# A fused linear-attention and gated-MLP kernel: another hand-written order of its operations, other queues for the first loads, and the last output block in two halves

## The chip, the cores and the metric

The kernel runs on one core of one Trainium2 chip. The metric is the time of one execution on the device in microseconds (us). An engine's name is followed by the short form that the profile uses: TensorE (PE; its weight loads PEld), VectorE (DVE), ScalarE (ACT), GpSimd (POOL) and SyncE (SP), which only issues DMAs.

## The reference

Inputs are float32: q, k, v of 8 batches x 8 heads x 576 tokens x 64, a feature matrix w_phi (64 x 128), and the MLP's weights w_in (512 x 1024), w_spatial (576 x 576), b_spatial and w_out (512 x 512).

```python
def phi(x):
    proj = np.einsum('bhsd,df->bhsf', x, w_phi)
    proj = proj - np.max(np.abs(proj), axis=-1, keepdims=True)
    return np.concatenate([np.exp(proj), np.exp(-proj)], axis=-1)
kv = np.einsum('bhsf,bhsd->bhfd', phi(k), v)
z = np.sum(phi(k), axis=2)
x = np.einsum('bhsf,bhfd->bhsd', phi(q), kv) / (np.einsum('bhsf,bhf->bhs', phi(q), z)[..., None] + 1e-06)
# heads side by side: x is batch x 576 x 512
h = np.maximum(x @ w_in, 0.0)
u, v = h[..., :512], h[..., 512:]
v_n = (v - mean(v)) / np.sqrt(var(v) + 1e-06)
v_s = np.einsum('ts,bsd->btd', w_spatial, v_n) + b_spatial[None, :, None]
out = (u * v_s) @ w_out
```

## The kernel before

A batch's 576 tokens are cut into 512 (four rows per partition, one descriptor each) and a tail of 64; the tails of two batches share 128 partitions. Every step is a small function (marked `@op`) named by a few letters; `ORDER` (line 17) is a text of some 1400 words, and the program is written out in just that order. A word such as `tkc.0.1.1:1@A` names the function, its arguments (batch, half or quarter, part), the buffer or PSUM bank after the colon, and the engine after the @ (A is ACT, V is DVE, P is POOL, S is SP). So the text alone decides what each engine does, in which order, in which of the buffers of `BUFS` (line 147), and which engine makes a copy; the framework adds the semaphores. Engines run their own rows strictly in order.

A batch goes through these steps.

- Loads: `lk` and `lq` (L358, L362) fetch k and q on POOL's queue, with the cast to bfloat16 on the way; `lv` (L388) fetches v on SP's queue, `lkt`, `lqt`, `lvt` (L271) the tails. Batch 0's k comes as four quarters of two heads each, in float32 (`lkf`, L348), each cast by `ckf` (L257) on DVE or POOL; its q comes as two halves (`lq0`, L372).
- Turning: `tk`, `tq` (L488) transpose on TensorE through PSUM, and `tkc`, `tqc` (L257 on DVE and POOL, L255 on ACT) copy the result to the tile T. Later batches use transposing DMAs instead (`xk`, `xq`, L474).
- Maxima: `kp`, `qp` (L540) multiply by w_phi, tokens on partitions; `km`, `qm` (L545, DVE) take the largest absolute value of each row and head.
- Features: `ke` (L549, ACT) takes the exponential of the key's product with both signs, `kem` and `kee` (L554) the exponential of the maxima; `vs` (L605, mostly POOL) multiplies v by the latter, and `kv` (L640, L642) sums on TensorE. For q the maxima are split into two bfloat16 (`qs`, L657, POOL), turned (`qt`, L662), copied (`qc`), and subtracted on TensorE while the product is made again (`qf`, L666, L670); `qe` (L675, ACT) takes the exponentials, `qn` (L724) multiplies by the sums and `qr`, `qx` (L730, L737, DVE) divide.
- MLP: x is turned (`tx`, L807, or `xx`, L800), `vm` and `um` (L839, L937) are the products with w_in, `vr`, `ur` their relu on ACT or DVE (L261, L263), `vb`, `va`, `vw`, `vn` the normalization, `sm` (L952, L954) the product along the tokens, `sg` (L961, DVE) the gate, `om` (L966) the product with w_out, `oc` (L255 or L257) the copy out of PSUM and `od` (L977) the store of one block of 128 tokens.
- `warm` (L334) issues matmuls whose result nobody reads; 35 of them stand in the first stages.

Batches overlap: products of the MLP of one batch stand between the attention of the next ones.

Of the kernel before, what the change touches and what calls it, by code (L numbers as in the profile page):

```python
# [53 lines left out]
kp.2.3:2,3 vnt.0.0:0@P kp.2.2:6,7 qp.3.0.1:0,1 vst.1.1.1:0@P qm.3.0.1:0 um.1.2:5 xk.3.0:5@S vm.1.3:4 ke.2.3.0:0
xk.3.1:3@S ke.2.2.0:3 km.2.3:3 km.2.2 vn.0.2@P xq.4.0:6@S ur.1.2:2@A vr.1.3:2@A ke.2.3.1 kee.2.0:2 vst.1.0.1@P tqt.1:0
vm.1.0:1 qt.2.1:4 qc.2.1:1@V vst.1.0.0@P tqtc.1:0@V spt.4:5 ke.2.2.1 vb.1.3:0 vr.1.0:1@A qp.3.1.0:2,3 vm.1.2:4
kee.2.1:3 qf.2.1.0:6,7 qf.2.1.1:0,1 vr.1.2:0@A qm.3.1.0:3 lk.4:0 vs.2.2.1:1@P spc.4@V qpt.1:2,3 qe.2.1.0.1:0
qe.2.1.0.0 sm.0.2:4 qmt.1:1 qe.2.1.1.1:4 qe.2.1.1.0 sm.0.3:5 vs.2.0.0:0@P sg.0.2 lout qp.3.0.0:2,3 qf.2.0.0:6,7
vsz.2.0@P vsz.2.2@P xq.4.1:1@S vbt.0.1:1 sm.0.1:4 qe.2.0.0.0:1 sg.0.3 qe.2.0.0.1 um.1.1:5 ur.1.1@A vb.1.0:3 qm.3.0.0
vb.1.2:2 qf.2.0.1:0,1 vsz.2.1:2@P vstz.1@P vs.2.2.0@P vs.2.3.1:3@P kp.3.0:2,3 qe.2.0.1.0:2 qp.3.1.1:6,7 sg.0.1  # L60
km.3.0:0 kv.2.2:5 kvc.2.2:2@V qe.2.0.1.1 vs.2.1.0@P qm.3.1.1 um.1.0:4 kp.3.1:0,1 km.3.1 um.1.3:5 ur.1.0@V ke.3.0.1:1
vat.0.1:2 qs.3.0:2@P vs.2.3.0@P sm.0.0:6 ke.3.0.0 vs.2.1.1@P vsz.2.3@P ur.1.3@A qt.3.0:7 qc.3.0:0@V kv.2.3:2 kv.2.1:3
ke.3.1.0:3 sg.0.0 ke.3.1.1 qp.4.0.0:4,5 vs.2.0.1@P vb.1.1:1 qs.3.1:0@P qst.1:2@P kp.3.2:6,7 kee.3.0:0 kvc.2.3@V
vsz.3.0:1@P kp.3.3:0,1 qm.4.0.0:2 smt.0.0:2 kvc.2.1@A vst.1.1.0@P lq.5:1 om.0.2:3 ke.3.2.0:0 sgt.0.0 ke.3.2.1 qt.3.1:2
qc.3.1:1@A qtt.1:4 kv.2.0:5 vs.3.0.0@P km.3.3:2 oc.0.2:0@A om.0.3:2 km.3.2 ke.3.3.0:2 qct.1:2@A kvc.2.0@V om.0.0:3
ke.3.3.1 oc.0.3:1@V qp.4.1.0:6,7 qf.3.0.0:4,5 lkt.2:1@S qn.2.0.0:0,1 oc.0.0:2@A qm.4.1.0:0 qr.2.0.0:1 va.1.2:3
xk.4.0:2@S qx.2.0.0:0 qn.2.1.0:2,3 vs.3.0.1@P qft.1:6,7 vs.3.1.0:3@P qn.2.0.1:0,1 vxt.0.1@V qr.2.1.0:2 vs.3.1.1@P
va.1.0 qe.3.0.0.0:3 qe.3.0.0.1 va.1.3 qx.2.1.0:1 va.1.1 ckt.2:0@P lk.5:2 qet.1.0:1 lv.4.0:1@S qet.1.1 qr.2.0.1:0
vx.1.2@V kee.3.1:3 qx.2.0.1 vsz.3.1@P qn.2.1.1:4,5 om.0.1:2 tx.2.1:3 qp.4.1.1:0,1 vy.1.2@V oc.0.1:3@A qr.2.1.1:1
txc.2.1:2@A xk.4.1:5@S qx.2.1.1 qm.4.1.1 vyt.0.1@V qf.3.0.1:6,7 qe.3.0.1.1:0 qp.4.0.1:4,5 qm.4.0.1 kv.3.0:2  # L70
vs.3.3.1:2@P vm.2.1:3 tx.2.2:0 tx.2.0:1 qe.3.0.1.0 kvc.3.0:0@V txc.2.2@A kp.4.0:4,5 ke.4.0.0:4 vw.1.2:2@P vn.1.2:2@P
vn.1.3@P vn.1.1@P qf.3.1.0:6,7 vr.2.1:0@V txc.2.0@V tkt.2:0 tx.2.3:2 txc.2.3@V vs.3.2.1:0@P qe.3.1.0.1:2 vm.2.2:1
qe.3.1.0.0 tktc.2:0@V vwt.0.1:3@P vsz.3.2@P vs.3.3.0@P km.4.0:1 vn.1.0@P vr.2.2:2@V vnt.0.1@P vm.2.0:2 vr.2.0:3@A
kv.3.1:0 ke.4.0.1 kp.4.2:6,7 kvc.3.1@A qf.3.1.1:2,3 vb.2.2:2 lv.4.1:3@S vb.2.0:3 vb.2.1:0 qs.4.1:0@P qe.3.1.1.1:4
lk.6:0 lvt.2:0@S vm.2.3:1 vs.3.2.0@P km.4.2:3 um.2.1:0 od.0.3@S vr.2.3:1@A qe.3.1.1.0 qs.4.0:2@P vsz.3.3@P smt.0.1:4
sgt.0.1 va.2.1:4 va.2.2 lv.5.1:0@S ur.2.1:0@V sm.1.2:1 kp.4.3:4,5 sg.1.2 kp.4.1:2,3 xq.5.1:3@S kv.3.2:0 km.4.3
# [75 lines left out]
def kernel(  # L152
# [16 lines left out]
    nc = tc.nc  # L169
# [5 lines left out]
    P = 128  # L175
# [886 lines left out]
```

## Time and profile before

| | us |
|---|---|
| median of 3 runs (lowest and highest) | 258.46 (257.28 to 258.59) |
| profiled execution | 259.11 |
| its span, from the first to the last record | 257.2 |
| TensorE busy in the span | 243.6 |
| VectorE busy | 218.4 |
| ScalarE busy | 194.5 |
| GpSimd busy | 155.7 |

HBM reads are 32.82 MB and writes 9.44 MB. In the rows of the timeline, the numbers are start and duration, then engine, line, operation and tiles; the bracket tells how long the engine was idle before it and what ended that. In the rows by stage each engine has its busy time and, in brackets, its instructions; behind them stand the granted TensorE clock (1 is full), the mean busy share of the 16 DMA engines and the GB/s that they moved. Rows of waits give the total, the times, and the longest. Spans of neighbouring instructions of one engine overlap a little at their ends.

### The profile page before, as it was taken

To read this page: it belongs to the slowest core of one execution; us is meant where nothing else is said; L and a number is where in the kernel's file an instruction comes from. 1 tells how busy PE (TensorE), PEld (TensorE's weight loads), DVE (VectorE), ACT (ScalarE), POOL (GpSimd) and SP (SyncE) were. 2 spreads that over 40 slices of the span, in tenths; PEclk is the share of its full clock that TensorE was granted. 3 is DMA by queue.
4 is the path that set the end of the run, shared out by engine and by line. 5 is a ranking of instruction groups with operands and counts; after the bars stand their busy time and mean duration, and the time that the engine had idled before them with its cause. 6 is when DMAs were issued, how large, how long until landed. Compare 5 with 4: busy or idle time off the path is not lost.

```text
span 257.2 us, 8031 instructions
## 1 busy us (share of the span) xinstructions
PE 243.6 (95%) x3256; PEld 150.0 (58%) x3293; DVE 218.4 (85%) x414; ACT 194.5 (76%) x303; POOL 155.7 (61%) x243
## 2 busy tenths in 40 slices
PE   7778999999999999999999999999999999999993
PEld 3345775786545676665575555566657665544541
DVE  4698999999999999999999999899997467857551
ACT  0698999999999999969998898968986812151422
POOL 3478995939988779689969552488992400242000
PEclk9997999999999999999999999999999999999999
DMA  6999999999799999777999999346521206322445
GB/s 157 257 223 242 211 194 170 298 154 203 102 145 187 259 220 140 105 138 110 155 181 217 242 178 247 100 105 164 166 41 28 59 4 132 115 82 82 159 159 212
DMA packets 77767, 40.79 MB, mean 159 GB/s; under 512 B 46754, under 2 KB 72994, under 8 KB 77732
## 3 DMA queue, kind: packets, MB, share of 16 engines
q1 hardware_dynamic: 59412, 29.37, 52.3%
q0 software_dynamic: 17424, 10.10, 29.4%
q10 hardware_dynamic: 896, 0.82, 1.0%
q8 instruction: 25, 0.41, 0.6%
q14 instruction: 10, 0.08, 0.1%
HBM read 32.82 MB, written 9.44 MB: 164 GB/s over the span
## 4 chain that ended last, share of the span: by engine, by line
PE 66%; DVE 14%; DMA 6%; issue 4%; POOL 4%; ACT 3%; ACTq 0%; POOLq 0%; DVEq 0%
PE banks L839 10%; PE banks L966 10%; PE banks L937 9%; PE banks L952 8%; DVE mq L545 5%; PE banks L540 5%; PE banks L640 5%; PE banks L724 4%; DMA T<-ld 4%; DMA ob<-in_k_dram 3%; PE banks L666 3%; PE banks L670 2%; ACT kf L549 2%; PE banks L954 2%; DVE x L737 2%
## 5 line engine op out<-in xcount | busy, mean ns | idle before, releaser
L675 ACT ACTIVATE qf<-banks 128x1024 bf16<-128x1024 f32 x72 | 70.5, 1037 | 6.5 <-PE banks L670 5.8
L605 POOL TENSOR_TENSOR vs<-v,em 128x512 bf16<-128x512 f32 x62 | 63.5, 1041 | 15.5 <-ACT em L554 13.3
L549 ACT ACTIVATE kf<-banks 128x1024 bf16<-128x1024 f32 x64 | 63.7, 1036 | 3.7 <-PE banks L839 1.1
L545 DVE TENSOR_REDUCE mk<-banks 128x8 f32<-128x1024 f32 x36 | 43.4, 1215 | 2.2 <-PE banks L540 1.8
L545 DVE TENSOR_REDUCE mq<-banks 128x8 f32<-128x1024 f32 x36 | 43.4, 1215 | 1.6 <-PE banks L540 1.5
L850 POOL TENSOR_TENSOR rs<-mv,neghalf 128x4 f32<-128x4 f32 (+2 forms) x13 | 11.5, 883 | 39.1 <-DVE mv L844 33.9
L952 PE MATMUL banks<-w_spT,vn 128*128 128x512 bf16 x118 | 32.2, 380 | 0.6
L937 PE MATMUL banks<-xT,w_u 128*128 128x512 bf16 x128 | 32.6, 379 | 0.0
L839 PE MATMUL banks<-w_v,xT 128*128 128x512 bf16 x115 | 31.2, 380 | 0.7
L966 PE MATMUL banks<-w_out,uT 128*128 128x512 bf16 x118 | 30.5, 379 | 0.7 <-issue 0.2
L255 ACT COPY ob<-banks 128x512 f32<-128x512 f32 x24 | 14.2, 596 | 19.1 <-PE banks L966 18.4
L961 DVE TENSOR_TENSOR uT<-banks,uT 128x512 bf16<-128x512 f32 x32 | 21.5, 684 | 7.6 <-PE banks L954 7.6
L540 PE MATMUL banks<-wphi,T 64*128 64x128 bf16 x512 | 24.0, 219 | 2.1 <-DVE mq L545 1.5
L640 PEld LDWEIGHTS <-kf 128*128 128x128 bf16 x512 | 22.0, 97 | 4.3 <-issue 0.5
L640 PE MATMUL banks<-vs,kf 128*128 128x66 bf16 x512 | 24.1, 194 | 0.3 <-POOL vs L605 0.2
L261 ACT ACTIVATE vr<-banks 128x512 bf16<-128x512 f32 (+1 forms) x22 | 13.4, 608 | 14.1 <-PE banks L839 13.8
L867 DVE BATCH_NORM_STATS2 st<-vr 128x6 f32<-128x512 bf16 x32 | 21.5, 681 | 1.6 <-ACT vr L261 1.4
L737 DVE TENSOR_TENSOR x<-banks,rc 128x512 bf16<-128x512 f32 x32 | 21.8, 686 | 0.6
L540 PEld LDWEIGHTS <-T 64*128 64x128 bf16 x512 | 15.9, 95 | 10.5 <-issue 7.3
L642 PE MATMUL banks<-vst,kft 128*128 128x66 bf16 x128 | 21.1, 191 | 0.0
L724 PE MATMUL banks<-kv,qf 128*128 128x66 bf16 x512 | 20.5, 193 | 0.1
L724 PEld LDWEIGHTS <-qf 128*128 128x128 bf16 x512 | 18.8, 97 | 3.0
(116 smaller groups left out, 448.4 us busy)
## 6 DMA issues: line engine op xcount, KB each, us to landing
v<-in_v_dram SPq DMA_DIRECT2D x16, 512.0 KB, 8.3
out_dram<-ob SPq DMA_DIRECT2D x32, 256.0 KB, 2.5
ld<-in_q_dram POOLq DMA_DIRECT2D x7, 512.0 KB, 8.7
ld<-in_k_dram POOLq DMA_DIRECT2D x7, 512.0 KB, 8.2
tf<-in_k_dram SPq DMA_DIRECT2D x8, 128.0 KB, 6.1
tf<-in_q_dram SPq DMA_DIRECT2D x8, 128.0 KB, 10.4
vt<-in_v_dram SPq DMA_DIRECT2D x8, 128.0 KB, 5.5
out_dram<-ob SPq DMA_DIRECT2D x8, 128.0 KB, 2.3
```

The source lines that it names most:

```text
L540: nc.tensor.matmul(out=bank(banks[y])[:, n * F:(n + 1) * F], lhsT=xT[halves[y], n, :], rhs=wphi[halves[y], :], start=True, stop=True)
L545: nc.vector.tensor_reduce(out=out_, in_=pp.rearrange("p y (n f) -> p y n f", f=F), axis=AX.X, op=ALU.max, apply_absolute_value=True)
L549: nc.scalar.activation(out=kf[:, s].rearrange("p y n f -> p y (n f)"), in_=pp, func=AF.Exp, bias=0.0, scale=(1.0, -1.0)[s])
L605: ENG[e].tensor_tensor(out=at["vs", (b, j)][:, s, :, 0:D], in0=at["v", (b, j // 2)][:, (j % 2) * n:(j % 2 + 1) * n, :], in1=at["em", (b, j ...
L640: nc.tensor.matmul(out=pv[:, hh, s, :], lhsT=kf[:, s, c % 2, 2 * hh + c // 2, :], rhs=w[:, s, NB * hh + c, :], start=(c == 0), stop=False)
L675: nc.scalar.activation(out=at["qf", u][:, s].rearrange("p y n t -> p y (n t)"), in_=at["pq", u], func=AF.Exp, bias=0.0, scale=(1.0, -1.0)[s])
L724: nc.tensor.matmul(out=at["pn", u][:, y, n, :], lhsT=f[:, s, y, n, :], rhs=at["kv", b][:, hg * HH + n, s, :], start=(s == 0), stop=(s == 1))
L737: nc.vector.tensor_tensor(out=at["x", (b, cc)][:, :, hg * HH:(hg + 1) * HH, :], in0=at["pn", u][:, :, :, 0:D], in1=at["rc", u].to_broadcas ...
L839: nc.tensor.matmul(out=bank(place)[r], lhsT=lhs[:, kc, r], rhs=w_v[:, kc, :], start=(kc == 0), stop=(kc == KC - 1))
L937: nc.tensor.matmul(out=bank(place).rearrange("p (c t) -> p c t", c=NB), lhsT=w_u[:, kc, dc * P:(dc + 1) * P], rhs=at["xT", b][:, :, kc, :] ...
L952: nc.tensor.matmul(out=bank(place), lhsT=at["vn", b][:, c, cs], rhs=w_spT[:, c, 0:T0], start=(c == 0), stop=False)
L966: nc.tensor.matmul(out=bank(place), lhsT=at["uT", b][:, dc, c * P:(c + 1) * P], rhs=w_out[:, dc, :], start=(dc == 0), stop=(dc == KC - 1))
```

## The change

`ORDER` is replaced by another text; `BUFS` and all steps stay as they are, except that the last output block is made by three new ones. The diff's core:

```diff
-zsp@V zmhl.2@V cident@P zvnt.0@V csel@V lkf.1:0@A lphi@A ckf.1:0@V lq0.4.4:1 warm.8:0 tk.0.0.1:0 tkc.0.0.1:0@V csel2@V
+zsp@V zmhl.1@V zvst.0@V zmhl.0@V lq0.4.4:0 lphi@A lkf.3:0@A lkf.1:1@S lkf.0:2@S lkt.0:0@S cident@P lq0.0.4 zvnt.0@V
...
+    ends = [slice(0, DM // 2), slice(DM // 2, DM)]
+
+    @op
+    def omh(e, b, c, y, place):
+        po = bank(place)[:, 0:DM // 2]
+        for dc in range(KC):
+            nc.tensor.matmul(out=po, lhsT=at["uT", b][:, dc, c * P:(c + 1) * P], rhs=w_out[:, dc, ends[y]],
+                             start=(dc == 0), stop=(dc == KC - 1))
+        at["po", (b, c, y)] = po
+
+    @op
+    def och(e, b, c, y, place):
+        copy(e, take("ob", (b, c, y), place)[:, ends[y]], at["po", (b, c, y)])
+
+    @op
+    def odh(e, b, c, y):
+        dst = bass.AP(tensor=out.tensor, offset=out.offset + (b * S + c) * DM + y * (DM // 2),
+                      ap=[[NB * DM, P], [1, DM // 2]])
+        ENG[e].dma_start(out=dst, in_=at["ob", (b, c, y)][:, ends[y]])
```

Counted over the whole table, 38 warm-up matmuls stand where 35 stood. Some copies change engines: the 32 copies of `kv` go from 16 on ACT to 23, the 5 of w_spT from 2 on DVE to 5, the products `vs` on DVE from 2 to 6, the normalizations `vn` on DVE from 10 to 7; one relu, 3 copies of the output, 3 of the turned maxima of the tails and 2 of x likewise go to DVE.

The first place is the queues of the first loads. SP's first rows before (in_k_dram into tf is a tail, into ob a quarter of batch 0's k; v_72 and v_73 are halves of batch 0's v):

```order
L271 DMA tf_77<-in_k_dram 64x8x64 x2
L348 DMA ob_163<-in_k_dram 128x2x256
L388 DMA v_72<-in_v_dram 128x4x256
L271 DMA tf_78<-in_q_dram 64x8x64 x2
L271 DMA vt_80<-in_v_dram 64x8x64 x2
L388 DMA v_73<-in_v_dram 128x4x256
```

And now:

```order
L348 DMA ob_161<-in_k_dram 128x2x256
L348 DMA ob_162<-in_k_dram 128x2x256
L271 DMA tf_77<-in_k_dram 64x8x64 x2
L388 DMA v_72<-in_v_dram 128x4x256
L271 DMA tf_78<-in_q_dram 64x8x64 x2
L271 DMA vt_80<-in_v_dram 64x8x64 x2
L388 DMA v_73<-in_v_dram 128x4x256
```

Two quarters of k stand ahead of the tail, one of them the quarter that is turned first. ACT's queue has w_phi and then the other two quarters, where it had a quarter, w_phi and two quarters.

POOL's first rows behind the constants, before (128x4x256 is a half of batch 0's q, 128x8x256 a whole batch of q or k, the casts make batch 0's k and tail):

```order
masks.py:199 AFFINE_SELECT ident<-ident 128x128
L372 DMA ld_63<-in_q_dram 128x4x256 x2
L257 CAST ld_62<-ob_161 128x512
L257 CAST ld_62<-ob_162 128x512
L257 CAST tl_76<-tf_77 128x512
L312 MEMSET neghalf 128x4
L257 CAST vs_95<-em_91 128x16x2
L362 DMA ld_64<-in_q_dram 128x8x256
L257 CAST ld_62<-ob_163 128x512
```

And now:

```order
L372 DMA ld_62<-in_q_dram 128x4x256
masks.py:197 MEMSET ident 128x128
masks.py:199 ISA
masks.py:199 AFFINE_SELECT ident<-ident 128x128
L372 DMA ld_62<-in_q_dram 128x4x256
L362 DMA ld_63<-in_q_dram 128x8x256
L257 CAST ld_64<-ob_160 128x512
L257 CAST ld_64<-ob_162 128x512
L257 CAST ld_64<-ob_163 128x512
L257 CAST tl_76<-tf_77 128x512
```

Batch 1's q is issued ahead of the casts, which wait for their loads; the first half of batch 0's q is issued ahead of the identity.

The second place is DVE's first rows from the first cast of k on (mk and mq are maxima of k and q, T, tT turned tiles, mT turned maxima). Before:

```order
L257 CAST ld_62<-ob_160 128x512
L257 COPY T_65<-banks 128x512
L307 TENSOR_SCALAR sel<-sel_169 128x1024
L257 CAST wphi<-wphi_f 64x128 x2
L545 TENSOR_REDUCE mk_87<-banks 128x2x4
L320 MEMSET vst_99 128x1056
L545 TENSOR_REDUCE mk_87<-banks 128x2x4
L257 COPY T_66<-banks 128x512
L257 COPY T_67<-banks 128x512
L257 COPY tT_79<-banks 128x512
L545 TENSOR_REDUCE mk_88<-banks 128x2x4
```

And now, where the memset of vst, sel and wphi stand ahead of these rows:

```order
L257 CAST ld_64<-ob_161 128x512
L257 COPY T_65<-banks 128x512
L545 TENSOR_REDUCE mk_87<-banks 128x2x4
L545 TENSOR_REDUCE mk_88<-banks 128x2x4
L257 COPY T_67<-banks 128x512
L257 COPY T_65<-banks 128x512
L257 COPY T_66<-banks 128x512
L257 COPY T_67<-banks 128x512
L545 TENSOR_REDUCE mk_87<-banks 128x2x4
L545 TENSOR_REDUCE mq_103<-banks 128x2x4
```

The second maximum is that of another quarter, whose turned tile ACT copies, and the setup has gone to the front.

The third place is the end of DVE's rows (ob is an output block in SBUF, uT the gated product). Before:

```order
L257 COPY ob_161<-banks 128x512
L961 TENSOR_TENSOR uT_157<-banks,uT_157 128x512 x2
L257 COPY ob_162<-banks 128x512
L257 COPY ob_164<-banks 128x512
L1057 UNCONDITIONAL_BRANCH
```

And now:

```order
L257 COPY vnt_154<-ident 128x512 x2
L961 TENSOR_TENSOR uT_157<-banks,uT_157 128x512 x3
L257 COPY ob_160<-banks 128x512
L257 COPY ob_162<-banks 128x512
L257 COPY ob_164<-banks 128x512
L257 COPY ob_163<-banks 128x256
L1077 UNCONDITIONAL_BRANCH
```

The last copy is one of 256 columns; ACT's last one is the other half, and ACT's queue issues the store of DVE's half. ACT's fill of vnt stands here on DVE.

More of the change, by code (lines that the diff above doesn't have):

```diff
@@ L73 @@
[L73 to L76, printed above, removed]
-ke.4.2.0:1 xq.5.0:4@S ke.4.2.1 va.2.0 ke.4.1.1:3 kv.3.3:1 kvc.3.2@V kvc.3.3@A km.4.1 sm.1.0:6 sg.1.0 cqt.2:0@P
@@ L143 @@
-oc.5.3:4@V od.5.3@S om.7.0:2 oc.7.0:2@A od.7.0@S
+zsp@V zmhl.1@V zvst.0@V zmhl.0@V lq0.4.4:0 lphi@A lkf.3:0@A lkf.1:1@S lkf.0:2@S lkt.0:0@S cident@P lq0.0.4 zvnt.0@V
+csel@V csel2@V cphi@V lq.1:1 ckf.3:2@P lkf.2:3@A ckf.1@V warm.10:0 tk.0.0.1:0 tkc.0.0.1:0@V warm.3:1 kp.0.1:2,3
+km.0.1:0 ckf.0@P tk.0.1.1:0 lv.0.0:0@S tkc.0.1.1:1@A warm.4:1 kp.0.3:4,5 km.0.3:1 warm.2:1 tk.0.0.0:0 ke.0.1.0:0
+warm.2:1 tq.0.1.0:1 ke.0.1.1 tq.0.1.1:6 ckf.2@P tqc.0.1.0:2@V ckt.0:0@P tkc.0.0.0@V kem.0.3:0 tk.0.1.0:7 tkc.0.1.0@V
@@ new lines @@
+warm.1:1 kp.0.0:2,3 tqc.0.1.1@V km.0.0 warm.1:1 qp.0.0.1:0,1 qm.0.0.1:0 warm.2:7 tq.0.0.1:6 ke.0.3.1:1 tqc.0.0.1:3@V
+ke.0.3.0 kem.0.1:1 tq.0.0.0:7 tqc.0.0.0@V ke.0.0.1:2 kem.0.0 ke.0.0.0 vsz.0.0:0@P chalf@P vsz.0.1:1@P lk.1:2
+kp.0.2:4,5 qp.0.1.1:0,1 tkt.0:6 ke.0.2.0:3 tktc.0:0@A qm.0.1.1:1 warm.2:7 qp.0.0.0:2,3 qm.0.0.0 lq.2:0 lin.0
+qs.0.0:1@P warm.2:7 qp.0.1.0:0,1 qm.0.1.0 warm.2:7 kpt.0:6,7 warm.2:2 tq.1.1.1:2 vs.0.0.0@P ke.0.2.1 qt.0.0:3 km.0.2
+tq.1.0.0:0 tq.1.1.0:1 lqt.0:1@S ket.0.0:0 tqc.1.1.0:4@V qs.0.1:0@P qc.0.0:0@A warm.2:3 qf.0.0.0:4,5 vs.0.1.1@P
@@ new lines @@
+om.1.3:1 lv.6.1:3@S vn.2.3@P xk.6.1:5@S xx.4.1:1@S ke.5.0.0:4 vb.3.3:0 od.1.2@S kee.5.0:1 vwt.1.2:0@P ke.5.0.1
+vs.5.1.0:3@P lk.7:2 qp.5.1.0:4,5 vs.5.2.0:1@P vnt.1.2:0@P qp.6.0.1:6,7 ur.3.2@A vr.3.2:0@V lv.7.1:1@S vb.3.1:3
+oc.1.3:3@A qf.4.0.1:2,3 om.1.1:0 vsz.5.2@P qm.5.1.0 vs.5.3.0@P qn.4.0.0:4,5 vs.5.1.1@P qm.6.0.1:0 qe.4.0.1.0:0
+qe.4.0.1.1 um.3.1:1 qr.4.0.0:0 qp.6.1.1:6,7 oc.1.1:0@A kp.6.1:2,3 qx.4.0.0:0 vsz.5.1@P ke.6.1.0:1 ke.6.1.1
+qf.5.0.1:4,5 ur.3.1@V sm.2.3:0 qe.5.0.1.1:2 xq.7.0:1@S qe.5.0.1.0 vb.3.2:1 qm.6.1.1:1 sm.2.1:1 sg.2.3 qn.4.0.1:6,7
```

231 lines of the change are left out of this document (112 added, 119 removed).

## The prediction, made before the changed kernel ran

> **What bounds the kernel now.** First the page's busy shares and its slices, to see which engine is full and from when.
>
> ```profile
> PE 243.6 (95%) x3256; PEld 150.0 (58%) x3293; DVE 218.4 (85%) x414; ACT 194.5 (76%) x303; POOL 155.7 (61%) x243
> ...
> PE   7778999999999999999999999999999999999993
> ...
> PEclk9997999999999999999999999999999999999999
> ```
>
> TensorE is full, except in the first four slices (25.7 us) and the last. In the fourth its granted clock is also down. So the share of 95% says nothing about the start; the stages do. Second view: busy time by stage.
>
> ```profile
> core 0: us, PE busy (x) PEld busy (x) DVE busy (x) ACT busy (x) POOL busy (x), PEclk, DMA share, GB/s
> 5.00:10.00 5.00, 3.62 (x28) 1.76 (x27) 3.54 (x6) 1.55 (x2) 0.61 (x1) 1.00 1.19 257
> 15.00:20.00 5.00, 3.22 (x40) 1.45 (x38) 4.87 (x8) 5.00 (x8) 4.67 (x8) 0.91 1.28 253
> 25.00:88.00 63.00, 61.39 (x997) 42.01 (x1004) 61.72 (x108) 61.16 (x98) 50.72 (x82) 1.00 1.18 192
> 100.00:140.00 40.00, 39.42 (x614) 25.32 (x620) 38.68 (x68) 37.02 (x60) 33.32 (x53) 1.00 1.01 144
> 140.00:200.00 60.00, 59.32 (x854) 36.85 (x864) 54.56 (x106) 50.31 (x75) 38.05 (x60) 1.00 0.63 146
> 200.00:253.00 53.00, 52.52 (x422) 27.31 (x428) 33.60 (x74) 18.37 (x33) 8.58 (x11) 1.00 0.34 107
> ```
>
> Three stages. To 25 us the loads and the chain behind them decide: the DMA share is over 1, and VectorE (DVE) and ScalarE (ACT) still wait. From 25 to about 88 us DVE is busy 61.72 of 63 us and ACT 61.16: a modelled-full TensorE there is partly one that is held up, and DVE, with least idle time, sets the pace. From 100 us TensorE is the bound (52.52 of 53 at the end, where ACT has 18.37). So time won before 25 us reaches the end only if DVE keeps it to 100 us, and every microsecond of work given to DVE before that point costs up to one.
>
> Third view: DVE's waits in the first 30 us, and the rows where they stand.
>
> ```profile
> DVE mk L545 <- PE banks L540: 1.6, 2, 1.1
> DVE ld L257 <- DMA ob<-in_k_dram: 1.4, 1, 1.4
> DVE T L257 <- PE banks L488: 1.4, 1, 1.4
> DVE w_spT L329 <- PEq L1046: 0.9, 1, 0.9
> DVE mq L545 <- PE banks L540: 0.8, 1, 0.8
> DVE T L257 <- ACT kf L549: 0.3, 1, 0.3
> ...
> 7.45 1.23 DVE L545 TENSOR_REDUCE mk<-banks 128x8 f32<-128x1024 f32 x1 [0.47 <-PE banks L540]
> ...
> 10.93 1.23 DVE L545 TENSOR_REDUCE mk<-banks 128x8 f32<-128x1024 f32 x1 [1.15 <-PE banks L540]
> ...
> 15.87 2.35 DVE L545 TENSOR_REDUCE mq<-banks 128x8 f32<-128x1024 f32 x2
> ```
>
> The waits sum to 6.4 us. Two maxima in a row take 2.35 us and one 1.23, so a further one costs DVE's queue some 1.13. The first comes at 7.45, the second not before 10.93, because its quarter of k lands late:
>
> ```profile
> 8.63 0.61 POOL L257 CAST ld<-ob 128x512 bf16<-128x512 f32 x1 [5.39 <-DMA ob<-in_k_dram]
> ...
> 6.08 1.28 ACT L255 ACT_TABLE_LOAD   x1 [6.08 <-DVE T L257]
> 9.73 0.59 ACT L255 COPY T<-banks 128x512 bf16<-128x512 bf16 x1 [2.37 <-PE banks L488]
> ...
> 11.88 0.89 POOL L362 DMA_DIRECT2D ld<-in_q_dram  x1
> ...
> ld<-in_q_dram POOLq DMA_DIRECT2D x1, 512.0 KB, 7.7
> ...
> DMA to landing us min/median/max: 3.0/7.5/9.2
> ```
>
> The last row is that of the four quarters of k: 3.0 us for the one issued first, 7.5 and more, up to 9.2, for those behind it. The two rows above it are batch 1's q: issued at 11.88, landed 7.7 us later, at 19.6.
>
> **The change part by part.** *Loads.* The first quarter moves from ACT's queue to the head of SP's, another goes to the head of ACT's behind the small w_phi, and the k tails stand behind two quarters instead of ahead. While three queues are busy they get equal packets:
>
> ```profile
> q0 software_dynamic: 469, 0.24, 44.3%
> q10 hardware_dynamic: 463, 0.45, 34.2%
> q1 hardware_dynamic: 491, 0.26, 28.2%
> ```
>
> That is 4 to 8 us, about 120 of 1 KB a microsecond and queue. A quarter has 256. First quarter and the one behind w_phi (64 packets) are then there by 3.8 to 4.5 us, the next two by 6 to 7.5, where now the last comes 9.2 us after its issue. GpSimd issues batch 1's q at 3 instead of 11.88; behind q0 (1024 packets) its 1024 end at 14 to 16 us, before TensorE asks for it at about 17.
>
> *DVE in the new order*, walked with these durations. Constants and w_phi now precede the first cast: 0.92 + 0.54 + 0.11 + 0.94 + 0.11 + 0.69 + 0.3 + 0.6 + 0.47 + 0.43 is 5.1 us. The first maximum follows after the same two waits as now (1.35 for the transposes, 0.47 for the product): about 7.2. ACT's table load hangs on DVE's copy (6.08 above, right behind it), so ends near 8.0; its copy of 0.59 and the product of 0.5 put the second maximum at 9.1, against 10.93. From there copies and maxima follow without a gap to 22, where the product of batch 1's q waits for its copies (0.55). Waits: 0.9 + 0.2 for the identity + 1.35 + 0.47 + 0.8 + 0.55 is 4.3 us, against 6.4. **Term 1: -2.1 us** (bounds: +0.5, if the megabyte of batch 1's q ahead of them makes v and the tails late, and -3, if the first copy follows its cast at full clock). ACT comes out only 1.1 us ahead in this walk, since kept from the second q features by TensorE's order at 21.5 to 22.9.
>
> *Work given to DVE.* Ahead of batch 4's keys (100 us) the table takes from ACT and GpSimd 3 copies of w_spT, one product v x em, 2 copies of T, 2 net of xT and 3 of mT, and gives back tl, 2 of kv and 2 of uT:
>
> ```profile
> L605 DVE TENSOR_TENSOR vs<-v,em 128x512 bf16<-128x512 f32 x2 | 1.5, 770 | 0.0
> ...
> L257 DVE COPY T<-banks 128x512 bf16<-128x512 bf16 x19 | 7.2, 414 | 2.1 <-PE banks L488 1.6 <-ACT kf L549 0.3
> ...
> L263 DVE TENSOR_SCALAR uT<-banks 128x512 bf16<-128x512 f32 x9 | 6.1, 673 | 0.4 <-PE banks L937 0.4
> ...
> L257 DVE COPY mT<-banks 128x128 bf16<-128x128 bf16 x11 | 2.4, 216 | 0.9 <-PE banks L662 0.7
> ...
> L257 DVE CAST kv<-banks 128x264 bf16<-128x264 f32 x16 | 6.7, 422 | 0.2
> ```
>
> With 0.45 for a copy of w_spT (estimate from T's 0.414): 1.35 + 0.77 + 0.83 + 0.83 + 0.65 - 0.42 - 0.84 - 1.35 is 1.8 us busy. Neighbours overlap by about 0.1 each (1.23 against 1.13), and some falls into DVE's own gaps (1.28 us in 25 to 88). **Term 2: +1.0 us** (0 to +1.8).
>
> *Warm-up matmuls.* 38 instead of 35; 3 x 0.22 = 0.65 us, beside waits of the first 17 us: nothing, at most +0.65. Two memsets move ahead of the first cast; counted above. One filling of vnt (2 x 0.4 us) goes from ACT to DVE near the end, where DVE has 33.60 of 53: nothing.
>
> *The last block.* Now 0.59 us of copy follow the last matmul, and then the store:
>
> ```profile
> 252.98 0.59 ACT L255 COPY ob<-banks 128x512 f32<-128x512 f32 x1 [1.14 <-PE banks L966]
> ...
> L1007 DVE TENSOR_TENSOR uTt<-banks,uTt 128x256 bf16<-128x256 f32 x8 | 3.3, 410 | 2.9 <-ACT ob L255 2.5 <-PE banks L1000 0.4
> ...
> out_dram<-ob SPq DMA_DIRECT2D x32, 256.0 KB, 2.5
> ...
> out_dram<-ob SPq DMA_DIRECT2D x8, 128.0 KB, 2.3
> ```
>
> The first half is copied beside the second's matmuls; the second, 256 columns on DVE, costs about 0.41, so -0.18; a store of half the size -0.1 to -0.2 (the two last rows). The columns add up to the same matmul time; four more weight loads overlap. **Term 3: -0.3 us** (0 to -0.4).
>
> Sum: -2.1 + 1.0 - 0.3 = -1.4 to -1.5. The profiled execution took 259.11 (span 257.2 and 1.9 around it), 0.65 over the median of 258.46; the sum against it gives 257.6, against the median **257.0 us**, which I take, since the result will be a median.
>
> **The rivals.**
>
> *The half-clock window comes back (about 258.0).*
>
> ```profile
> 15.68:19.09 3.41, 1.85 (x28) 0.92 (x27) 3.41 (x4) 3.41 (x7) 3.33 (x7) 1.00 1.28 273
> 19.09:22.51 3.42, 3.17 (x30) 1.84 (x32) 2.46 (x4) 2.23 (x6) 2.94 (x3) 0.50 1.30 236
> ...
> 21.24 1.02 ACT L675 ACTIVATE qf<-banks 128x1024 bf16<-128x1024 f32 x1 [1.19 <-PE banks L670]
> ```
>
> After 3.41 us with 1.85 busy the clock is 0.50 for 3.42 us; in it ACT waits 1.19 and DVE 0.8. The new table pairs each product of 12 to 17 us with two warm-ups, about 0.7 of every 1.13 us. But in my walk TensorE stands at 19.8 to 22.3 behind a copy of batch 1's q. If that counts as sparse, products, q features and kv sums of about 3 us fall into 3.4 us at half speed: +1.0. The Trainium skill, "TensorE: Matmul & The Clock Gate", section "HAM oscillation — how this bites in real kernels", asks only that no idle gap exceed about 3.4 us; by it neither table would lose its clock and this rival would vanish. The trace disagrees: in the 3.41 us ahead of the fall TensorE was busy for 1.85, so no gap was that long. The measurement decides, and the rival stays.
>
> *DVE stays the bound for longer: slower (about 259.9).* Ahead of batch 6's keys DVE's instructions sum to 4.6 us more than before (2.3 of them maxima pulled forward), TensorE's to 1.0 more. Its idle time in 100 to 140 us is 1.32. If that cannot be used up, 4.6 - 1.0 - 2.1 = 1.5 us remain, and with them lost 258.46 + 1.5, about 259.9. It decides from the point where DVE is gapless up to about 150 us; against it speaks that 140 to 200 us leaves DVE 5.4 us.
>
> *The early lead passes whole (about 255.3).* If the given work vanishes in gaps and the clock stays up, ACT's 1.19 us are saved too: -2.1 - 0.8 - 0.3.
>
> *Nothing early (about 258.2):* the loads share one DMA bandwidth, the DMA share stays over 1 to 40 us, and batch 1's q lands at 19.6 as now; only the tail remains. I count it with the first rival.
>
> **How the numbers follow.** Forecast 0.42, half clock or no lead 0.29, DVE bound 0.20, whole lead 0.09. A measurement tells about 0.5% from no change: 257.17 to 259.75. Forecast and whole lead lie mostly below (0.46 in sum), the first rival mostly between (0.31 with the forecast's rest), the third mostly above (0.23 with some stall I don't see). Range 255.2 to 260.0, from the whole lead to the extended DVE bound; it leaves out some 0.2.
>
> **What would show it.** Right: second maximum near 9.1, DVE's waits to 30 us near 4.3, clock 1.00 through 26 us, DVE over 61 of 63 in 25 to 88. Wrong: GpSimd's first cast still at 8, a wait of TensorE for batch 1's q after 17 us, clock 0.50 after 22 us, TensorE waiting for DVE beyond 100 us.

## The result, and the profile after

The changed kernel takes 259.87 us (median of 8 runs, 259.02 to 260.78) where the kernel before takes 257.57 (8 runs beside them, 256.61 to 258.59): a ratio of 1.0068, 95% interval 1.0042 to 1.0094. It is slower: by 2.3 us between the medians, by 1.8 (1.1 to 2.4) by the ratio; the forecast was 257.0, lower than before. The profiled execution took 260.78, its span 258.9.

The page of the changed kernel: busy time, and the slices of TensorE and its clock.

```profile
PE 246.4 (95%) x3300; PEld 150.1 (58%) x3300; DVE 224.0 (87%) x424; ACT 191.2 (74%) x295; POOL 153.4 (59%) x242
...
PE   7997999979999999999998999999999999999992
...
PEclk9999999999999999999999999999999999999999
```

The dip of the clock in the fourth slice is gone, though TensorE still has a 7 there. But slices 9 and 22 (6.47 us each: 51.8 to 58.2 and 135.9 to 142.4 us) have a 7 and an 8 for TensorE, where before no slice between the fourth and the last was under 9. Busy time by stage shows the size of both (columns as in the prediction):

```profile
15.00:20.00 5.00, 4.95 (x53) 2.49 (x54) 5.00 (x7) 4.93 (x8) 4.72 (x10) 1.00 1.13 164
25.00:88.00 63.00, 60.70 (x966) 40.54 (x963) 60.27 (x108) 59.36 (x93) 50.41 (x77) 1.00 1.18 191
...
140.00:150.00 10.00, 8.85 (x120) 5.15 (x118) 9.00 (x17) 7.89 (x11) 8.91 (x14) 1.00 1.18 214
150.00:200.00 50.00, 50.00 (x694) 30.35 (x694) 44.33 (x84) 42.77 (x66) 28.49 (x47) 1.00 0.50 123
200.00:253.00 53.00, 53.00 (x491) 28.67 (x486) 37.05 (x85) 16.30 (x28) 10.77 (x13) 1.00 0.35 97
```

15 to 20 us is filled as was meant: 4.95 of 5 for TensorE, 3.22 before. Yet in 25 to 88 us TensorE, DVE and ACT are all less busy than before (DVE 60.27, where it was 61.72 and the prediction asked for over 61), and TensorE loses 1.15 us in the ten from 140 to 150.

The start went about as the prediction walked it. DVE's first maxima in the changed kernel:

```profile
7.64 1.22 DVE L545 TENSOR_REDUCE mk<-banks 128x8 f32<-128x1024 f32 x1 [0.69 <-PE banks L540]
9.41 1.23 DVE L545 TENSOR_REDUCE mk<-banks 128x8 f32<-128x1024 f32 x1 [0.55 <-PE banks L540]
```

9.1 was expected for the second. DVE's waits to 30 us sum to 3.6 us; 4.3 was expected.

### The profile page after: what moved, and what is told of

Read it like the earlier page. It is cut to its first block, busy times and chain, and to the rows that moved or that the text cites. A ratio compares the mean times of both kernels' runs of the same rounds, so it can differ in the third digit from the quotient of the medians.

```text
span 258.9 us, 8080 instructions
## 1 busy us (share of the span) xinstructions
PE 246.4 (95%) x3300; PEld 150.1 (58%) x3300; DVE 224.0 (87%) x424; ACT 191.2 (74%) x295; POOL 153.4 (59%) x242
## 4 chain that ended last, share of the span: by engine, by line
PE 69%; DVE 12%; DMA 7%; issue 4%; POOL 3%; ACT 3%; ACTq 0%; DVEq 0%; POOLq 0%
PE banks L839 11%; PE banks L937 9%; PE banks L952 9%; PE banks L966 7%; PE banks L640 6%; PE banks L540 5%; PE banks L724 4%; DMA T<-ld 4%; DVE mq L545 3%; PE banks L666 2%; DVE mk L545 2%; DMA ob<-in_k_dram 2%; PE banks L954 2%; PE banks L670 2%; POOL vs L605 2%
## 5 line engine op out<-in xcount | busy, mean ns | idle before, releaser
L605 POOL TENSOR_TENSOR vs<-v,em 128x512 bf16<-128x512 f32 x58 | 59.7, 1043 | 7.5 <-ACT em L554 4.0
L952 PE MATMUL banks<-w_spT,vn 128*128 128x512 bf16 x128 | 32.9, 379 | 0.3 <-DVE uTt L1027 0.3
L839 PE MATMUL banks<-w_v,xT 128*128 128x512 bf16 x128 | 32.1, 379 | 0.0
L255 ACT COPY ob<-banks 128x512 f32<-128x512 f32 (+1 forms) x22 | 12.8, 585 | 19.7 <-PE banks L966 12.5
L640 PEld LDWEIGHTS <-kf 128*128 128x128 bf16 x512 | 22.0, 97 | 4.1 <-issue 0.6
L640 PE MATMUL banks<-vs,kf 128*128 128x66 bf16 x512 | 23.7, 194 | 0.1
L853 POOL TENSOR_SCALAR vn<-vr,mv,rs 128x512 bf16<-128x512 bf16 x25 | 19.5, 781 | 4.6 <-DVE mv L847 4.0
L642 PE MATMUL banks<-vst,kft 128*128 128x66 bf16 x128 | 21.0, 191 | 0.3 <-issue 0.3
L724 PEld LDWEIGHTS <-qf 128*128 128x128 bf16 x512 | 18.9, 98 | 3.8 <-issue 0.3
L724 PE MATMUL banks<-kv,qf 128*128 128x66 bf16 x512 | 20.8, 193 | 0.3 <-DVE x L737 0.3
```

The costliest lines, as they stand in the source:

```text
L605: ENG[e].tensor_tensor(out=at["vs", (b, j)][:, s, :, 0:D], in0=at["v", (b, j // 2)][:, (j % 2) * n:(j % 2 + 1) * n, :], in1=at["em", (b, j ...
L640: nc.tensor.matmul(out=pv[:, hh, s, :], lhsT=kf[:, s, c % 2, 2 * hh + c // 2, :], rhs=w[:, s, NB * hh + c, :], start=(c == 0), stop=False)
L724: nc.tensor.matmul(out=at["pn", u][:, y, n, :], lhsT=f[:, s, y, n, :], rhs=at["kv", b][:, hg * HH + n, s, :], start=(s == 0), stop=(s == 1))
L839: nc.tensor.matmul(out=bank(place)[r], lhsT=lhs[:, kc, r], rhs=w_v[:, kc, :], start=(kc == 0), stop=(kc == KC - 1))
L952: nc.tensor.matmul(out=bank(place), lhsT=at["vn", b][:, c, cs], rhs=w_spT[:, c, 0:T0], start=(c == 0), stop=False)
```

## The experiments

The version that has one edit, the later load of batch 7's keys, is the base of the later ones; it is called "keys later". Ratios stand against runs of the kernel before on the same chip.

### GpSimd's queue at 138 us (k7_later)

GpSimd and TensorE of the changed kernel, around the loss at 140 us:

```profile
134.61 1.03 POOL L605 TENSOR_TENSOR vs<-v,em 128x512 bf16<-128x512 f32 x1
138.92 0.98 POOL L358 DMA_DIRECT2D ld<-in_k_dram  x1 [3.28 <-DMA T<-ld]
139.93 1.05 POOL L605 TENSOR_TENSOR vs<-v,em 128x512 bf16<-128x512 f32 x1
140.97 1.62 POOL L853 TENSOR_SCALAR vnt<-vr,mv,rs 64x512 bf16<-64x512 bf16 x2
```

```profile
139.66 1.04 PE L952 MATMUL banks<-w_spT,vn 128*128 128x512 bf16 x4
141.78 0.39 PE L954 MATMUL banks<-w_spT,vnt 128*128 128x512 bf16 x1 [1.08 <-POOL vnt L853]
```

The new order puts `lk.7`, the load of batch 7's keys, ahead of a product and two tail normalizations. The buffer that it loads into, `ld` number 2, held batch 6's queries (`lq.6:2`), and a transposing DMA (`xq.6.0`) still reads it; until that lands GpSimd stands for 3.28 us, and everything behind the load stands with it, though its inputs are there. Before, the same load came after this work.

```diff
- vs.5.1.0:3@P lk.7:2 qp.5.1.0:4,5 vs.5.2.0:1@P vnt.1.2:0@P
+ vs.5.1.0:3@P qp.5.1.0:4,5 vs.5.2.0:1@P vnt.1.2:0@P lk.7:2
```

> The changed kernel with the load of batch 7's keys issued by GpSimd three instructions later, behind a product v x em and the two tail normalisations of batches 4 and 5 (2.5 us of work that stood behind a wait of 3.3 us). Theory GPSIMD (TensorE's 1.3 us lost at 140 to 150 us come from the work queued behind this load): 258.7 us, about 1.2 below 259.87, and TensorE's wait for vnt is gone. Theory DVE BOUND (VectorE, not GpSimd, sets the pace to 150 us): no difference, 259.9, another wait takes its place.

(The normalizations are those of batches 2 and 3; the expectation names other batches.) Measured: 258.23 us, ratio 1.0017 (0.9991 to 1.0043), so 1.6 us below the changed kernel by the medians and 1.3 by the ratios. GpSimd of this version, then TensorE:

```profile
135.89 1.62 POOL L853 TENSOR_SCALAR vnt<-vr,mv,rs 64x512 bf16<-64x512 bf16 x2
137.80 0.98 POOL L358 DMA_DIRECT2D ld<-in_k_dram  x1 [0.29 <-issue]
```

```profile
139.78 0.38 PE L954 MATMUL banks<-w_spT,vnt 128*128 128x512 bf16 x1
```

The normalizations run 5.1 us earlier and the load is issued 1.1 us earlier (0.7 of both stems from a shorter halt at 53 us, below); TensorE's wait for them is gone. The two profiles stand 0.7 us apart up to 140 us, 2.0 from this matmul on (141.78 against 139.78) and 2.2 at the end, so 1.3 to 1.5 of it is the load's. That is the larger part of the loss, and it speaks against a VectorE that is the bound up to 150 us: nothing of VectorE's was touched.

### The last block (tail_same_buf, tail_whole, before_halves, k7_tail)

In the changed kernel the copy of the last half waits 2.08 us for a store, 1.0 of it after the half's matmuls:

```profile
253.19 1.04 PE L985 MATMUL banks<-w_out,uT 128*128 128x256 bf16 x8
...
255.30 0.42 DVE L257 COPY ob<-banks 128x256 f32<-128x256 f32 x1 [2.08 <-DMA out_dram<-ob]
```

Its buffer, number 3 of five, was being stored from: that store was issued at 251.41 us. The first edit below puts the second half into the buffer of the first.

```diff
- och.5.0.1:3@V
+ och.5.0.1:0@V
```

> The changed kernel with one digit changed: the second half of the last block goes into output buffer 0, beside the first half, instead of buffer 3. Theory BUFFER (the copy of the second half waited 2.08 us for the store that still read buffer 3, of which 1.0 us came after its matmuls): 258.8 us, 1.0 below the changed kernel's 259.87; its copy starts within 0.1 us of the last matmul's end. Theory of the prediction (the halves gain 0.3 us as they stand, the loss lies earlier): no difference, 259.9.

```diff
- omh.5.0.0:6 omh.5.0.1:0 ... och.5.0.0:0@A odh.5.0.0@S och.5.0.1:3@V odh.5.0.1@A
+ om.5.0:6 ... oc.5.0:0@A od.5.0@S
```

> The changed kernel with its last block whole again (one group of four matmuls, one copy by ScalarE, one store). Theory BUFFER: the halves as placed cost more than they save, 259.3 to 259.5 us (0.4 to 0.6 below 259.87). Theory of the prediction: 260.2 us (0.3 above).

```diff
- om.7.0:2 oc.7.0:2@A od.7.0@S
+ omh.7.0.0:2 omh.7.0.1:0 och.7.0.0:2@A odh.7.0.0@S och.7.0.1:2@V odh.7.0.1@A
```

> The kernel before with nothing but its last block in two halves of the columns, both in the one buffer that the block had. The prediction's third term: 0.3 us below the kernel before (257.57), 257.3 us. Theory HALVES COST (the eight short matmuls and the second store take what the shorter copy saves): no difference, 257.6.

Measured: 259.23 us with one buffer for both halves (ratio 1.0066, 1.0035 to 1.0098), 260.03 with the whole block (1.0073, 1.0039 to 1.0106), and 257.83 for the kernel before with halves (0.9999, 0.9967 to 1.0032). With one buffer the copy is 0.9 us earlier:

```profile
253.12 1.04 PE L985 MATMUL banks<-w_out,uT 128*128 128x256 bf16 x8
...
254.39 0.42 DVE L257 COPY ob<-banks 128x256 f32<-128x256 f32 x1 [1.24 <-DMA out_dram<-ob]
```

but the span is 258.8, against 258.9: it ends 4.0 us after that copy instead of 3.2. The time from issue to landing of the last store, that of DVE's half, tells why. First the changed kernel, where it is issued at 255.76 us, then one buffer, issued at 254.84:

```profile
out_dram<-ob ACTq DMA_DIRECT2D x1, 128.0 KB, 2.1
```

```profile
out_dram<-ob ACTq DMA_DIRECT2D x1, 128.0 KB, 3.0
```

It lands at 257.8 us in both, 1.0 ahead of the span's end. Other stores are in flight beside it, so the stores, and not the last copy, set the end here. The same edit upon "keys later":

> The version with the later load of batch 7's keys (258.23 us), and the second half of the last block in output buffer 0 beside the first. Theory BUFFER: 257.2 to 257.7 us (the copy's 1.0 us of waiting behind its matmuls goes; alone the edit measured 0.6). Theory NO MATTER (the last stores, not the copy, set the end): 258.2.

258.34 us (1.0039, 1.0015 to 1.0064): no gain. Nothing that the halves gain can be told from noise, and neither can a cost of the wait for the buffer. Theory BUFFER fell.

### Which start the kernel before has (before_halves again, before_warm)

The kernel before with halves has the old order up to its last block, so its profile is a second execution of the old start. It begins unlike the profile that the prediction read: GpSimd's first cast and DVE's second maximum stand at

```profile
7.49 0.61 POOL L257 CAST ld<-ob 128x512 bf16<-128x512 f32 x1 [4.26 <-DMA ob<-in_k_dram]
```

```profile
9.78 1.23 DVE L545 TENSOR_REDUCE mk<-banks 128x8 f32<-128x1024 f32 x1
```

and not at 8.63 and 10.93, since a quarter of k landed 1.1 us earlier; and no half-clock window follows. From 22 us on every product and maximum of this execution stands 2.1 us earlier than in the one shown, and stays so to the end of the span (255.1 against 257.2). Busy time to 26 us, the kernel before as profiled first, this second execution of its start, and the changed kernel:

```profile
0.00:26.00 26.00, 20.41 (x208) 11.27 (x210) 19.28 (x36) 16.37 (x28) 15.64 (x31) 0.93 1.09 220
```

```profile
0.00:26.00 26.00, 21.08 (x258) 12.32 (x262) 21.16 (x38) 18.41 (x31) 17.67 (x35) 1.00 1.13 217
```

```profile
0.00:26.00 26.00, 22.04 (x248) 11.93 (x248) 22.51 (x38) 18.52 (x31) 16.55 (x36) 1.00 1.11 199
```

By its busy time, DVE's lead at 26 us is 22.51 - 19.28 = 3.2 us against the first execution, and 22.51 - 21.16 = 1.35 against the second. Which is usual? One window of 3.41 us at half clock in a span of 257 us makes a mean clock of 0.993, which is what the first execution has. Of 102 executions of the kernel before that ran beside the first four sets of experiments, 45 have a mean clock under 0.9955 (median 258.07 us), 57 one above (257.00); the share of the former differs between the chips, from 2 of 16 to 19 of 35. The profile shown, 259.11 us, was of the kind with the lower clock, and late even among those. Can two more warm-ups keep the clock up?

```diff
- warm.1:4 qp.0.0.0:4,5
+ warm.3:4 qp.0.0.0:4,5
```

> The kernel before with two more warm-up matmuls (0.43 us) in the sparsely filled stretch at 14.5 us, ahead of the product whose maximum VectorE reaches 0.7 us after it is ready. In 19 of 35 runs of the kernel before on the first chip the mean clock is under 0.9955 and the median 258.28, in the other 16 it is 257.19. Theory CLOCK (a half-clock window of 3.4 us from a thinly filled stretch makes that difference): mean clock 0.998 or more in nearly all runs, and a median about 0.5 us below that of the kernel before in the same job, near 257.1. Theory NO CLOCK (the slower runs come from elsewhere, the first loads for instance): the same share of runs under 0.9955 and no gain, or a loss of up to 0.4.

257.31 us, ratio 1.001 (0.9991 to 1.0029); no execution of 12 is below 0.996, but on this chip only 2 of 16 of the kernel before were. Undecided.

### Parts of the change alone (before_loads, k7_engines, k7_give)

```diff
- lkf.1:0@A lphi@A ckf.1:0@V ... lkf.0:1@A lq0.0.4 ... lkf.3:2@A ... lkt.0:0@S ... lkf.2:3@S ... lq.1:2
+ lphi@A lkf.3:2@A lkf.1:0@S lkf.0:1@S lkt.0:0@S ckf.1:0@V ... lq0.0.4 lq.1:2 lkf.2:3@A
```

> The kernel before with nothing but its first loads in the changed kernel's order and queues (two quarters of batch 0's k at the head of SyncE's queue, two behind w_phi on ScalarE's, the tail behind them, batch 1's q ahead of GpSimd's casts). The prediction's first term at its full size: 255.5 us, 2.1 below the kernel before (257.6). Theory SLOW START (the profiled execution of the kernel before started 2.1 us later than others of the same kernel do, so the term was measured against an exception): 256.6 us, about 1.0 below. Theory BANDWIDTH (the loads share one rate anyway): 257.6.

259.27 us, ratio 1.0064 (1.0033 to 1.0094): slower by 1.5, which none of the three had. GpSimd's cast of the tail of k, then DVE's copy of it:

```profile
12.75 0.61 POOL L257 CAST tl<-tf 128x512 bf16<-128x512 f32 x1 [6.05 <-DMA tf<-in_k_dram]
```

```profile
13.86 0.42 DVE L257 COPY tT<-banks 128x512 bf16<-128x512 bf16 x1 [2.17 <-PE banks L516]
```

The old order turns the tail early; with the new loads it lands late, and GpSimd, TensorE and DVE wait in turn. A half-clock window follows, from 14.88 to 18.30 us in the profile, and 9 of the 12 executions have a mean clock under 0.9955. So the new loads lose in the old order of the work; what they gain in the new one was not measured apart from it.

For the second term, the engine letters of all 37 tasks ahead of batch 4's keys went back (21 leave VectorE, 16 return to it), then of four tasks only:

> The version with the later load of batch 7's keys (258.23 us), with the engine letters of the kernel before in all tasks ahead of batch 4's keys (37 small copies, relus and products go back to the engine that had them). The prediction's second term (work given to VectorE costs 1.0 us): 257.2 us. Theory EVEN (VectorE and ScalarE are about equally full there, and the copies stand where the new order has room for them): no gain, 258.2 us or above.

```diff
- vs.0.2.0@V ... spc.2@V ... spc.0@V ... spc.3@V
+ vs.0.2.0@P ... spc.2@A ... spc.0@A ... spc.3@A
```

> The version with the later load of batch 7's keys (258.23 us), and four of the tasks that the change gave to VectorE ahead of 63 us given back to the engine that had them, in their new places: three copies of w_spT (1.3 us) to ScalarE and one product v x em (0.77 us) to GpSimd. The prediction's second term (work on VectorE costs up to its own length there): 1.0 to 2.0 us less, 256.2 to 257.2. Theory EVEN (the other engines have no room at these places either): no gain or a loss, 258.2 to 260.

273.73 us (1.0636, 1.0606 to 1.0667), and 259.04 (1.0072, 1.0044 to 1.0099). With all letters of before, TensorE is busy 17.64 of 22 us in 26 to 48, where "keys later" has 21.55, and from 38.45 to 45.27 us its clock is 0.50, which the changed kernel has nowhere; so the 15 us are no price of VectorE's work. With four, new waits take the place of the work: of TensorE for a copy now on ACT and a product now on GpSimd:

```profile
PE banks L640 <- POOL vs L605: 0.5, 1, 0.5
PE banks L488 <- ACT w_spT L255: 0.5, 1, 0.5
```

So, in these two trials, the letters belong to the places in the order, and what VectorE was given can't be priced by taking it back.

### A halt without a wait, at 53 and 30 us

The other new dip is this, TensorE of the changed kernel:

```profile
53.13 0.39 PE L540 MATMUL banks<-wphi,tT 64*128 64x128 bf16 x7
54.57 0.21 PE L540 MATMUL banks<-wphi,tT 64*128 64x128 bf16 x1 [1.05 <-issue]
```

Seven of eight matmuls of one group run, the eighth comes 1.26 us after the seventh (0.06 is usual). It waits for no semaphore, and "issue" says that the profile shows no cause. The page lists 26 packets on a queue of their own:

```profile
q8 instruction: 26, 0.43, 0.7%
```

They have 16 KB each. TensorE has 6600 recorded instructions (3300 matmuls, 3300 weight loads), so a packet would hold some 254 of them. In the trace's single packets, one of the 26 started at 50.69 us and took 2.30 us, where most take about 1.0.

```diff
- xk.3.1:4@S urt.0:0@A ... lv.3.0:1@S ... lv.2.0:3@S
+ urt.0:0@A ... lv.3.0:1@S ... lv.2.0:3@S xk.3.1:4@S
```

> The version with the later load of batch 7's keys (258.23 us), and one transposing DMA of batch 3's k issued by SyncE behind two loads of v instead of ahead of them (some 3 us later; its turned tile is read 15 us after it landed). Theory FETCH (TensorE's halt at 53.3 us, 0.62 to 1.35 us in all four profiles of this table with no wait on the halted instruction, is a late fetch of its instructions, held up by this DMA's packets of 1.4 to 1.5 us): the halt is gone, 257.4 us, 0.6 to 1.0 lower. Theory ORDER (the halt belongs to the instructions that stand there): the halt stays at 0.6 or more, 258.2.

258.76 us (1.0051, 1.0027 to 1.0074), a halt of 0.40 us from one matmul to the next, and long packets of 1.4 us still there: the transposing DMA that I suspected is not what makes the packets long. But six profiles with this start line up the end of that instruction packet and the halted matmul:

| profile | packet ends | eighth matmul | after the seventh |
|---|---|---|---|
| k7_tail | 51.91 | 53.47 | 0.12 |
| k7_xk | 52.09 | 53.71 | 0.40 |
| k7_later | 52.56 | 53.84 | 0.62 |
| changed kernel | 52.99 | 54.57 | 1.26 |
| tail_same_buf | 53.20 | 54.65 | 1.29 |
| tail_whole | 53.47 | 54.78 | 1.35 |

The matmul starts 1.3 to 1.6 us behind the packet's end in all six, however long the halt. If TensorE waits for a block of instructions, the place depends on the count of instructions ahead, and moves when some are taken out or put in at the start:

```diff
- warm.10:0
+ warm.8:0
```

> The version with the later load of batch 7's keys (258.23 us), and 8 instead of 10 warm-up matmuls at the very start: two matmuls and two weight loads fewer ahead of everything else. Theory FETCH (TensorE's instructions come in blocks, and the halt at 53.3 us is the wait for a block): if the halt shows, it is no longer ahead of the eighth matmul of the L540 group but two matmuls later, ahead of the second of the L778 group behind it; ahead of that matmul by 0.1 to 1.3 us. Theory ORDER (something that the eighth matmul itself needs): it stays ahead of the eighth. Time: 258.2 either way, since TensorE waits for data there.

> As the one above with 6 instead of 10 warm-up matmuls at the start (four matmuls and four weight loads fewer). Theory FETCH: the halt, if it shows, stands ahead of the fourth matmul of the L778 group. Theory ORDER: ahead of the eighth of the L540 group. Time: 258.2, or 259 if the clock falls without them.

258.88 us (1.0046, 1.0016 to 1.0075) and 259.55 (1.0082, 1.0054 to 1.0109). At 53 us there is no halt in either; TensorE comes to that place only at 54.9 and 55.6 us, 2.5 and 2.9 us behind the end of the packet. The halt at 30 us tells more: in the changed kernel it is ahead of the 55th matmul of the sums with v (L640, L642), with six warm-ups, so four matmuls fewer, ahead of the 59th. First the changed kernel, then six warm-ups:

```profile
30.05 0.29 PE L640 MATMUL banks<-vs,kf 128*128 128x66 bf16 x4
30.67 0.19 PE L642 MATMUL banks<-vst,kft 128*128 128x66 bf16 x1 [0.33 <-issue]
```

```profile
31.73 0.26 PE L640 MATMUL banks<-vs,kf 128*128 128x66 bf16 x3
32.88 0.19 PE L640 MATMUL banks<-vs,kf 128*128 128x66 bf16 x1 [0.88 <-issue]
```

These two start 1.40 and 1.42 us behind the end of their packets (29.27 and 31.46 us). With eight warm-ups there is a small one, a step of 0.25 us where 0.03 is usual, ahead of the 57th.

Then the other way, with small matmuls in front:

```diff
+    def tiny(e, n, place):
+        for i in range(n):
+            nc.tensor.matmul(out=bank(place)[:, 0:16], lhsT=w_spT[:, NB + 1, 0:P], rhs=w_spT[:, NB, 0:16], start=True, stop=True)
...
- warm.10:0
+ tiny.24:0 warm.8:0
```

> The version with the later load of batch 7's keys (1.0017 of the kernel before), where 24 matmuls of 16 columns take the place of two of the ten warm-ups at the very start: 44 more TensorE instructions ahead of everything else, at about the same time of the first product (estimate from 0.43 us for a warm-up there). Theory FETCH: the places at which TensorE can halt move 22 matmuls towards the start; a halt at 30 us, if there is one, stands ahead of the 33rd matmul of the sums with v (55th before), that at 53 us inside the L724 group; since slower matmuls then stand behind the fetch that is late, halts sum to 0.5 us or less, and the time is 0.998 to 1.001 of the kernel before. Theory ORDER: halts ahead of the 55th and ahead of the eighth of L540 as before.

> As above with 48 matmuls of 16 columns for four of the ten warm-ups: 88 more instructions, places 44 matmuls towards the start. Theory FETCH: a halt at 30 us stands ahead of the 11th matmul of the sums with v, that at 53 us in the sums with v of batch 2 or the transposes; sum of halts 0.5 us or less, 0.998 to 1.001 of the kernel before, unless the start is later because small matmuls don't bring the clock up (then up to 1.4 us more, as with six warm-ups alone). Theory ORDER: halts at the same two instructions.

(48 of them go with warm.6.) With 24, the halt at 53 us stands 22 matmuls earlier, as expected, inside another group (L729 is what L724 is in the others):

```profile
52.78 0.19 PE L729 MATMUL banks<-kv,qf 128*128 128x66 bf16 x1
53.30 0.64 PE L729 MATMUL banks<-kv,qf 128*128 128x66 bf16 x15 [0.32 <-issue]
```

It starts 1.45 us behind the end of its packet (51.85). The time is 257.99 us (1.0028, 1.0002 to 1.0055), above what was expected. With 48 there is no halt (TensorE comes to the place 3.3 us behind the end of the packet), and 257.38 us: 1.0002 of the kernel before (0.9975 to 1.0029), span 255.1. Some 0.25 us of that is an earlier start: its run of four maxima of q starts at 22.35 us, where "keys later" has it at 22.60 (full clock from 5.21 us and from 7.17). So what the halts alone cost isn't separated.

The count from the program's start says it best. In the changed kernel and with six warm-ups, the matmul halted at 30 us and at 32.88 us has 352 recorded weight loads ahead of it; in the six profiles of the table and with 24 small matmuls, the one halted at 53 us has 736. Which matmul that is differs with the instructions in front, the count does not. Between the two places lie 384 weight loads and as many matmuls, 768 instructions, which is three times 256. That TensorE waits there for a block of its instructions is thus well supported; what makes that packet late is open.

The Trainium skill, "Runtime: NRT & Kernel Launch", section "Instruction fetch mechanics", says that instructions come in blocks of 16 KiB, 256 of them, and that crossing a block costs a bump of a queue that is mostly hidden. The size agrees with the 26 packets; the cost doesn't here, where TensorE issues some 45 recorded instructions a microsecond (128 from 50.69 to 53.52 us) and the DMA engines are full (a share of 1.58 in that stretch).

## Why the prediction was wrong

*Term 1, -2.1.* The step that failed first: "Waits: [...] is 4.3 us, against 6.4". The 6.4 us belong to an execution that was late by 2.1 us, 1.1 for a quarter of k and 1.0 for the half clock; with the start of the second execution the same waits are 4.9. Part of what was to be gained, many executions of the kernel before have already. The walk of the new order was nearly right: second maximum 9.41, clock 1.00, GpSimd's first cast at 7.11, waits 3.6; batch 1's q landed at 16.8, later than the 14 to 16 said, and still ahead of the 17 at which it was needed. (The rate behind that, 120 packets a microsecond and queue, holds; 1 KB a packet holds for q10 alone, the rows of q0 and q1 give half of it.) Against the other start DVE's lead was 1.35 us. To set the sum "against the median [...], which I take", and not against the execution's own 259.11, made it worse: the median had part of that gain in it. That median was of three runs, too; that of the eight is 257.57.

*Term 2, +1.0.* Its size was not measured alone. "Keys later" with 48 small matmuls, which has no halts, ends level with the kernel before (1.0002), so what the new order costs and the lead of 1.35 us about cancel; that all of this cost is work given to DVE is not shown. That "every microsecond of work given to DVE costs up to one" is no way to price single tasks: given back, four of them cost 0.8 us more (259.04 against 258.23; 1.4 by the ratios) instead of 1 to 2 less.

*Warm-ups, 0.* The three more were not tried alone; two more in the kernel before cost nothing that shows (1.001). But in the new order the ten at the start are worth some 0.7 us (1.0046 with eight, 1.0017 with ten): with eight, TensorE idles 1.08 us and runs at half rate (0.61 for a group that takes 0.40) up to 10 us. Eight warm-ups, then ten ("keys later"):

```profile
6.18 0.61 PE L488 MATMUL banks<-ident,ld 128*128 128x128 bf16 x4 [1.08 <-DVE ld L257]
...
8.01 0.61 PE L540 MATMUL banks<-wphi,T 64*128 64x128 bf16 x8
```

```profile
5.88 0.61 PE L488 MATMUL banks<-ident,ld 128*128 128x128 bf16 x4
...
7.47 0.40 PE L540 MATMUL banks<-wphi,T 64*128 64x128 bf16 x8
```

*Term 3, -0.3.* No gain was measured (0.9999, 0.9967 to 1.0032; 0.3 us, or 0.0012, would lie within the interval). In the changed kernel the span ends with the landing of the stores, and an earlier last copy didn't bring it forward: the store behind it took 3.0 us instead of 2.1.

*What no term had*, and what turned the gain into a loss. I walked the order only to 100 us, on the ground that from there TensorE is the bound and only the lead matters. A bound engine still stands when another is made late: GpSimd's load, at 139 us, costs 1.3 to 1.6. And the halts, 0.1 to 1.3 us at 53 us, have no row in a trace of the kernel before.

Set against the medians: 259.87 - 258.23 = 1.6 for the load, and 258.23 - 257.57 = 0.66 for all the rest: what the new order, the halts and a late full clock cost, less the lead of 1.35. "Keys later" can't be told from the kernel before (0.9991 to 1.0043), so the rest isn't split further.

*The rivals.* "DVE stays the bound for longer" gives 259.9, the measured time, by luck. DVE is indeed nearly full for longer (39.35 of 40 us in 100 to 140, 44.33 of 50 in 150 to 200). But from 100 us to the end the waits that the profile lists for TensorE are 1.1 us for GpSimd and 0.3 for DVE, and most of the loss went when a load of GpSimd was moved. The half clock did not come back: it is 1.00 in the profile from 6.6 us to the end.

## What to carry to other kernels

Where the start of a kernel depends on loads, read its start from several executions before pricing what could be gained there; in two executions of the kernel before, an offset of 2.1 us at 22 us stayed to the end. In a change of order, look at each load that moves ahead of work on an engine that executes in order, and ask who still reads the buffer it fills, also in stages where that engine has time to spare. Letters and places of a hand-made order belong together: the new loads in the old order lost 0.6%, the old engine letters in the new order 6%.

## What the runs showed of the hardware

TensorE can halt at an instruction that waits for no semaphore: 0.1 to 1.3 us, always behind the same count of its instructions (352 or 736 weight loads), 1.3 to 1.6 us behind the end of a 16 KB instruction packet; 22 matmuls more or 4 fewer in front moved the place by as many. And idle time ahead of the full clock cost more than itself: with eight warm-ups, 1.08 us of it at 5.1 us, the full clock came at 10.0 us, where eight profiles with ten warm-ups have it at 4.3 to 7.3, and the maxima stand 1.4 us later than in "keys later" from there on. The kernel before, with eight warm-ups and no such gap right behind them, had the full clock from 5.3 to 5.5 us in three profiles.
